# Sparse attention and a bilinear FFN on one core: a fifth pair of seven products, in four PSUM banks

## The chip, the core and the metric

The kernel runs on one core of one Trainium2 chip. The time is the device time of one execution in microseconds; the text works in microseconds from the start of the profiled span where it names a moment. Engines are called PE (TensorE, matmuls), DVE (VectorE), ACT (ScalarE), POOL (GpSimd) and SP (SyncE, which only issues DMAs here). Each engine works through its own queue in the order in which the program wrote it.

## What is computed

Attention for 8 batches of 576 tokens with 8 heads of 64, then a feed-forward block over all 4608 tokens:

```python
scores = scale * np.matmul(q, k.transpose(0, 1, 3, 2))
mask_local = (rel >= 0) & (rel < 32)                    # heads 0 to 3
mask_strided = (rel >= 0) & (pos[None, :] % 32 == pos[:, None] % 32)   # heads 4 to 7
attn = softmax(np.where(mask, scores, -1e9));  x = attn @ v
a = x @ w_a;  b = x @ w_b                               # 512 -> 1536
out = (a * b) @ w_out                                   # 1536 -> 512
```

Matmuls take bf16 inputs and sum in fp32.

## The kernel before

**Tiles and slots.** The 4608 tokens are nine tiles of 512, t = 0 to 8. Each tile has 16 slots: 12 slots f for the columns of a and b (128 features each), then 4 slots for y, the product with w_out. The attention of batch b = t + 1 is cut into small steps that are put between and inside the slots of tile t, in an order that the tables `PAIRED`, `IN_P` and `IN_Y` write out by hand for tiles 2 to 6 (`MID_A`). What a slot issues goes straight into the engines' queues; there is no scheduler behind it.

**A regular slot f** (`ffn_ab`) is four matmuls of 128x128 by 512 tokens for a and four for b, a copy of a on ACT, and a multiplication a * b on DVE into `pf`.

**A pair by seven products** (`a_pair_mid`, pairs g = 0 to 5 are slots 2g and 2g + 1). For two slots, a is a 2x2x2 block product: two blocks of features, two halves of the 512 inputs (256 each), two halves of the tokens. It is done with seven products in place of eight, each of two matmuls of 256 tokens; b stays as it is, with eight matmuls of 512. The products need sums of weight blocks (`wsum_make`, made once in tiles 1 and 2) and of token blocks (`xsum_make`, per tile). Four quarters of a are put together from the products by copies on ACT and adds on DVE; by the numbering in `a_pair`'s plan

    a(0, first half)  = 1 + 2          a(0, second half) = 1 + 6 + 5 + 3
    a(1, first half)  = 1 + 6 + 7 + 4  a(1, second half) = 1 + 6 + 5 + 7

Before, pairs 1 to 4 of tiles 2 to 6 run so, in five PSUM banks: X (products 1, 6, 5, 3 summed up one after the other, and copied out after each), Y (product 2), Z (7, then 4), and b0, b1 for b. Three adds of 256 follow. Pairs 0 and 5 are regular slots.

**PSUM.** Eight banks: three `mm` and one `tp`, handed out in turn by `mm_bank`; `o` and `e`; and `st`, two banks for scores. A bank is given out again when the last reader of its former use is done.

**Attention steps.** `s` makes the scores of a unit u (PE) and their Exp (ACT), `m` masks them (DVE, L417). Units 0 to 3 are local heads, 4 to 7 strided ones. `V` of a strided unit (`step_VT`) multiplies with v into banks `o` and `e` (PE, L519, four matmuls into each), takes Ln of the sums on ACT (L531, one for each bank), Exp of the negative (L532), and multiplies on DVE into `xT` (L534, one for each bank). Units 4 and 5 stand at the ends of slots 9 and 11, unit 6 and 7 inside y.

**The work before y.** y is done by seven products too. `fast_s(t, n, groups)` makes the sums of `pf` for it on DVE (L829): n = 0, 1, 2, 3, for groups of pairs. Sum 1 is made from sum 0. In y, the products run in the order 1, 7, 6, 4, 5, 2, 3; product 1 needs `pf` itself, 7 needs sum 2, 6 needs sum 1.

**POOL** issues the loads of k, q and v; a one-element copy `pace` of the slot's result ahead of a slot's steps holds them back. Other lines named later: L646 and L649 are copy and multiplication of a regular slot, L695 the matmuls of the seven products, L709 those of b, L714 the multiplications, L717 the adds, L721 to L738 the copies, L668 the weight sums, L895 the matmuls of y, L862 and L864 its adds on DVE, L460 the products of a local unit.

Of the kernel before, what the change touches and what calls it, by code (L numbers as in the profile page):

```python
# [7 lines left out]
F32 = mybir.dt.float32  # L8
# [25 lines left out]
def kernel(  # L34
# [10 lines left out]
    nc = tc.nc  # L45
# [218 lines left out]
    def pair_up(nm, c):  # L264

        if (nm, c) == ("k", 1):
            t = shared[1][:96, -RL * 128:]
        else:
            t = blocks(*{"k0": "q0", "q0": "q1", "q1": "k0"}[f"{nm}{c}"])
            t = t.rearrange("p h n -> p (h n)")[:96, :RL * 128]  # L270
        nc.vector.tensor_copy(by_row(t), nats[1, nm, False][:, 2 * c:2 * c + 2])
        paired[1, nm, c] = t.rearrange("p (r m) -> p r m", r=RL)
# [233 lines left out]
        nc.sync.dma_start(out=xT[:, c, S * (b % XR):S * (b % XR + 1)], in_=scratch.pop((b, c)), transpose=True)  # L506

    def step_VT(b, u):

        c, half, M, n, G = unit(u)  # L510
        p = ps.pop((b, u))
        if "e" in psum4:
            o = [psum4[nm].tile([128, 512], F32, tag=nm, name=nm) for nm in "oe"]
        else:
            o2 = psum4["o"].tile([128, 2, 512], F32, tag="o", name="o")
            o = [o2[:, j] for j in range(2)]
        for j in range(2):
            for i in range(G):
                nc.tensor.matmul(o[j][:, i * n:(i + 1) * n], lhsT=vs_buf[b % 2][:, u - HL, 2 * i + j],  # L519
                                 rhs=p_cols(b, p, j, i, n, n)[:M], start=True, stop=True)  # L520
        r = sb.tile([128, RS * 4 * D], BF16, tag="xr", name="xr", bufs=2)[:64, :4 * W].bitcast(F32)
        by_token = lambda t: t.rearrange("d (p i j) -> d p i j", i=G, j=2)
        dst = xT[64 * (u % 2):64 * (u % 2) + 64, c, S * (b % XR):S * (b % XR + 1)]
        if "e" not in psum4:
            by_j = lambda t: t.rearrange("d j (i p) -> d p i j", p=NP)
            nc.scalar.activation(by_token(r), by_j(o2[64:, :, :W]), ACT.Ln)
            nc.scalar.activation(r, r, ACT.Exp, scale=-1.0)
            nc.vector.tensor_mul(by_token(dst), by_j(o2[:64, :, :W]), by_token(r))
            return
        for j in range(2):  # L530
            nc.scalar.activation(by_token(r)[:, :, :, j], o[j][64:, :W].rearrange("d (i p) -> d p i", p=NP), ACT.Ln)  # L531
        nc.scalar.activation(r, r, ACT.Exp, scale=-1.0)  # L532
        for j in range(2):
            nc.vector.tensor_mul(by_token(dst)[:, :, :, j], o[j][:64, :W].rearrange("d (i p) -> d p i", p=NP),  # L534
                                 by_token(r)[:, :, :, j])
# [30 lines left out]
    def F_mm(f, w, kk):  # L566
# [20 lines left out]
             11: "V5"}  # L587
    IN_Y = {2: "S7", 6: "V6", 11: "V7"}
    PAIRED = {-4: "Q0", -3: "Q1", -1: "S0", 0: "S1", 1: "V0 Q2", 2: "s2", 3: "V1 Q3 O0", 4: "s3", 5: "V2", 6: "s4", 7: "V3 O1 I0", 8: "s5",
              9: "V4 I1", 10: "s6", 11: "m6 V5"}  # L590
    IN_P = {1: "m2", 2: "m3", 3: "m4", 4: "m5"}
    FN = {"Tk": step_Tk, "Tq": step_Tq, "S": step_S, "V": step_V, "X": step_X, "W": lambda b, n: fast_w(n, slice(0, 3)),
          "s": S_px, "m": S_m, "L": lead_vl, "O": rows_out, "I": rows_in, "Pk": lambda b, c: pair_up("k", c), "Pq": lambda b, c: pair_up("q", c),
          "Q": lambda b, n: step_Q(b, n // 2, n % 2)}

    def run(b, slot):
# [85 lines left out]
    def a_pair_mid(t, g):  # L682

        pf = pfs[t]
        r = [mm_bank([128, TTOK]) for _ in range(4)]
        r.append(psum4["e"].tile([128, 512], F32, tag="e", name="e"))
        Y, X, Z, b1, b0 = [r[i] for i in ((0, 2, 4, 1, 3), (0, 4, 1, 2, 3), (0, 1, 2, 4, 3))[(g - 1) % 3]]
        X, Y, Z = X[:, :HT], Y[:, :HT], Z[:, :HT]
        a = [fsb.tile([128, TTOK], F32, tag="a_sb", name="a_sb", bufs=4) for _ in range(2)]
        p7 = fsb.tile([128, HT], F32, tag="p7", name="p7")  # L690
        quarter = lambda e, k: a[e][:, HT * k:HT * (k + 1)]

        def P(bank, lhs, rhs, start=False):
            for c in range(2):
                nc.tensor.matmul(bank, lhsT=lhs(c), rhs=rhs(c), start=start and c == 0, stop=c == 1, skip_group_check=True)  # L695

        w = lambda e, j: (lambda c: wav[:, j, c, g, e])
        ws = lambda n: (lambda c: wsum_a[n][:, c, g])
        x = lambda j, k: (lambda c: x_part(t, j, k)[:, c])
        xs = lambda n: (lambda c: xsum[t][:, n, c])  # L700

        def b_mm(bank, e, kks):
            f = 2 * g + e
            x0 = TTOK * t % (XR * S)
            for kk in kks:
                for k in range(2) if x0 + TTOK > XR * S else (None,):
                    rhs = x_part(t, kk // 2, k)[:, kk % 2] if k is not None else xT[:, kk, x0:x0 + TTOK]
                    dst = bank if k is None else bank[:, HT * k:HT * (k + 1)]
                    nc.tensor.matmul(dst, lhsT=wb_sb[:, kk, 128 * f:128 * (f + 1)], rhs=rhs,  # L709
                                     start=kk == 0 and k in (None, 0), stop=kk == KD - 1 and k in (None, 1))  # L710

        def mult(e, bank):
            halves = lambda v_: v_.rearrange("p (a i s) -> p a i s", i=2, s=16)
            nc.vector.tensor_mul(pf[:, 2 * g + e, :].rearrange("p (i a s) -> p a i s", i=2, s=16), halves(a[e]), halves(bank))  # L714

        def add(q, other):
            nc.vector.tensor_tensor(q, other, q, op=ALU.add)  # L717
# [268 lines left out]
    with tc.manual_schedule(engines={ENG.PE, ENG.SP, ENG.Pool, ENG.DVE, ENG.Activation}):  # L986
# [193 lines left out]
```

## Time and profile before

| | us |
|---|---|
| timed runs: median (lowest, highest of 3) | 321.04 (318.89, 322.53) |
| the profiled execution: its time | 318.67 |
| its span in the profile | 317.0 |
| PE busy, in 2770 matmul records | 308.2 |
| DVE busy | 263.7 |
| ACT busy | 198.3 |
| POOL busy | 112.0 |

The granted PE clock is 1.000 over the whole span. Matmul records overlap, since matmuls are pipelined: the time between the starts of two is what one costs. Busy times of DVE and ACT are durations of instructions, and two that follow each other overlap by up to 0.1. Some 28 of 2798 matmuls have no record.

### The profile page before, as it was taken

Reading aid. Unit: us, or ns where it says so; the run is one execution under the profiler, and the core shown is the slowest. Engines: PE = TensorE matmul, PEld = TensorE weight load, DVE = VectorE, ACT = ScalarE, POOL = GpSimd, SP = SyncE. Lnnn points to the kernel's source line nnn. Section 1 sums busy time; section 2 is a strip of 40 time slices with the busy share of each in tenths; the row PEclk is TensorE's granted clock in tenths of the full one; section 3 lists DMA queues with packets and bytes.
Section 4 is the critical chain, followed back from the end, with each engine's and each line's share of the span. In section 5 each row is a group of like instructions: output and inputs, shape, how many; then the busy total and the mean of one; then the engine's idle time right before and its main releaser. Section 6 shows DMA issues by size and latency. Waiting matters only on the chain. (4 is left out here: it accounts for less than half of the span.)

```text
span 317.0 us, 7353 instructions
## 1 busy us (share of the span) xinstructions
PE 308.2 (97%) x2770; PEld 220.6 (70%) x2798; DVE 263.7 (83%) x594; ACT 198.3 (63%) x414; POOL 112.0 (35%) x186
## 2 busy tenths in 40 slices
PE   7899999999999999999999999999999999999994
PEld 6754565455866687767999986769676966786684
DVE  6887876698979998999799978997899768847862
ACT  7964776455766776567666765686667755435541
POOL 8935712772263164115421434133101112203520
PEclk9999999999999999999999999999999999999999
DMA  9999999999799999999999999899352040004004
GB/s 159 168 205 202 203 184 202 216 104 172 127 137 148 223 144 81 127 228 134 108 114 225 118 130 106 202 138 134 30 154 58 0 135 0 2 0 133 2 0 134
DMA packets 127059, 40.32 MB, mean 127 GB/s; under 512 B 114864, under 2 KB 124144, under 8 KB 126832
## 3 DMA queue, kind: packets, MB, share of 16 engines
q0 software_dynamic: 79760, 19.20, 65.2%
q1 hardware_dynamic: 47120, 20.59, 38.8%
q8 instruction: 22, 0.36, 0.5%
q14 instruction: 13, 0.11, 0.1%
q10 hardware_dynamic: 144, 0.07, 0.1%
HBM read 38.93 MB, written 18.28 MB: 181 GB/s over the span
## 5 line engine op out<-in xcount | busy, mean ns | idle before, releaser
L625 PE MATMUL mm<-xT,wb_sb 128*128 128x512 bf16 (+1 forms) x189 | 46.8, 361 | 0.4
L625 PE MATMUL mm<-xT,wa_sb 128*128 128x512 bf16 (+1 forms) x183 | 46.1, 360 | 0.2
L1146 POOL CAST pace<-pf 1x1 f32<-1x1 bf16 x46 | 14.5, 316 | 81.1 <-DVE pf L714 31.6
L399 ACT ACTIVATE p<-st 72x576 bf16<-72x576 f32 (+1 forms) x56 | 36.4, 650 | 9.1 <-PE st L379 8.2
L709 PE MATMUL mm<-xT,wb_sb 128*128 128x512 bf16 (+1 forms) x160 | 38.0, 342 | 0.4
L646 ACT COPY a_sb<-mm 128x512 f32<-128x512 f32 x44 | 25.7, 583 | 15.7 <-PE mm L625 14.9
L895 PEld LDWEIGHTS <-ps 128*128 128x128 bf16 x336 | 32.7, 98 | 3.7
L625 PEld LDWEIGHTS <-wb_sb 128*128 128x128 bf16 x192 | 18.2, 98 | 16.8 <-DVE pf L714 0.3
L895 PE MATMUL mm<-wf,ps 128*128 128x256 bf16 x252 | 29.8, 273 | 0.0
L860 ACT COPY y_sb<-mm 128x512 f32<-128x512 f32 (+1 forms) x32 | 17.9, 558 | 19.0 <-PE mm L895 16.4
L649 DVE TENSOR_TENSOR pf<-a_sb,mm 128x512 bf16<-128x512 f32 x34 | 23.1, 680 | 5.9 <-ACT a_sb L646 5.8
L625 PEld LDWEIGHTS <-wa_sb 128*128 128x128 bf16 x192 | 17.4, 98 | 12.4
L1146 POOL COPY pace<-y_sb 1x1 f32<-1x1 f32 x22 | 8.4, 380 | 49.9 <-DVE y_sb L858 27.3
L895 PEld LDWEIGHTS <-pf 128*128 128x128 bf16 x252 | 23.5, 98 | 2.7
L775 PE MATMUL mm<-xT,wb_sb 128*128 128x512 bf16 x83 | 25.3, 379 | 0.1
L709 PEld LDWEIGHTS <-wb_sb 128*128 128x128 bf16 x192 | 18.7, 97 | 7.4
L238 POOL DMA_DIRECT2D vs<-in_v_dram x24 | 21.7, 907 | 3.9 <-ACT y_sb L860 1.3
L714 DVE TENSOR_TENSOR pf<-a_sb,mm 128x512 bf16<-128x512 f32 x35 | 22.7, 683 | 0.5
L895 PE MATMUL mm<-wo_sb,pf 128*128 128x256 bf16 x168 | 21.8, 273 | 0.0
L829 DVE TENSOR_TENSOR ps<-pf 128x512 bf16<-128x512 bf16 (+2 forms) x37 | 17.8, 481 | 0.7
L460 PEld LDWEIGHTS <-p 128*128 128x128 bf16 (+1 forms) x256 | 12.9, 97 | 5.2 <-DVE p L417 1.3
L417 DVE TENSOR_TENSOR p<-p,mask_l 128x576 int16<-128x576 int16 x32 | 14.4, 451 | 2.2 <-ACT p L399 2.0
(222 smaller groups left out, 734.2 us busy)
## 6 DMA issues: line engine op xcount, KB each, us to landing
out_dram<-y_sb SPq DMA_DIRECT2D x14, 512.0 KB, 4.8
kr<-in_k_dram POOLq DMA_DIRECT2D x12, 288.0 KB, 6.1
qr<-in_q_dram POOLq DMA_DIRECT2D x12, 288.0 KB, 8.1
vl<-in_v_dram POOLq DMA_DIRECT2D x6, 384.0 KB, 6.9
out_dram<-y_sb SPq DMA_DIRECT2D x7, 256.0 KB, 4.3
vs<-in_v_dram POOLq DMA_DIRECT2D x24, 72.0 KB, 5.7
xd<-xl SPq DMA_DIRECT2D x12, 144.0 KB, 4.0
wo_sb<-in_moe_w_out_dram POOLq DMA_DIRECT2D x4, 384.0 KB, 11.7
```

The costliest lines, as they stand in the source:

```text
L238: nc.gpsimd.dma_start(out=vs_buf[b % 2][:, h, :, 0:D], in_=v[b, HL + h].rearrange("(p r) d -> p r d", r=RS))
L399: nc.scalar.activation(p_flat(p)[:M, :2 * W].rearrange("p (i n) -> p i n", n=2 * n), st[:M].rearrange("p a (i n) -> p (a i) n", n=256)[:, ...
L625: nc.tensor.matmul(ps_[:, c0:c0 + n], lhsT=w[:, kk, 128 * f:128 * (f + 1)], rhs=xT[:, kk, x0:x0 + n], start=(kk == first and c0 == 0), sto ...
L646: nc.scalar.copy(a_sb, ab[0])
L649: nc.vector.tensor_mul(pf[:, f, :].rearrange("p (i a s) -> p a i s", i=2, s=16), halves(a_sb), halves(ab[1]))
L709: nc.tensor.matmul(dst, lhsT=wb_sb[:, kk, 128 * f:128 * (f + 1)], rhs=rhs, start=kk == 0 and k in (None, 0), stop=kk == KD - 1 and k in (N ...
L714: nc.vector.tensor_mul(pf[:, 2 * g + e, :].rearrange("p (i a s) -> p a i s", i=2, s=16), halves(a[e]), halves(bank))
L775: nc.tensor.matmul(got[e], lhsT=wb_sb[:, kk, 128 * f:128 * (f + 1)], rhs=xT[:, kk, x0:x0 + TTOK], start=kk == 0, stop=kk == KD - 1)
L829: nc.vector.tensor_tensor(s[:, n], a, b, op=op)
L860: nc.scalar.copy({"1": part(0, 0), "7": part(0, 1), "6": part(1, 0), "5": part(1, 1)}[k], bank)
L895: nc.tensor.matmul(bank[b][:, q], lhsT=lhs(g, q), rhs=rhs(g), start=k in "172" and q == 0 and g == 0, stop=g == FG - 1, skip_group_check=True)
L1146: nc.gpsimd.tensor_copy(pace, done)
```

## The change

- **Pair 5** of tiles 2 to 6 becomes a pair by seven products like pairs 1 to 4. The weight sums for pair 5, so far made in tile 2's y, are made with those of pairs 1 to 4 in tile 1.
- **Four banks.** Products 2 and 5 go side by side into one bank W, product 3 onto 5. X takes 1, 6, 7 and 4, summed up and copied out after each. One add of 512 (W onto a(0)) and one of 256 (u3 = 1 + 6 + 7 onto a(1)) replace the three adds. The first half of the pair now does b0 with the products 1, 2, 5, 6, 3, 7, the second half b1 with product 4; the multiplication for feature block 0 (`mult(0, b0)`) stands at the start of the second half. Bank `e` serves pairs 1 to 3 alone. Which bank has which part is written out for each pair.
- **Strided unit 4 in parts**: `u` (products and the two Ln) at the end of slot 9, `x` (Exp) inside pair 5 behind the copy of product 6, `n` (the two multiplications on DVE, which free banks `o` and `e`) at the end of slot 10. The other strided units call the three parts one after the other.
- **Sums for y**: sum 1 of groups 0 to 3 moves from slot 10 to slot 9, behind sum 2 of these groups; sum 2 of groups 4 and 5 moves into pair 5, behind `mult(0, b0)`.

```diff
-MID_A = {t: (1, 2, 3, 4) for t in (2, 3, 4, 5, 6)}
+MID_A = {t: (1, 2, 3, 4, 5) for t in (2, 3, 4, 5, 6)}
...
     def step_VT(b, u):
+        VT_p(b, u)
+        VT_x(b, u)
+        VT_n(b, u)
...
+    def VT_x(b, u):
+        r = held[b, "vt", u][3]
         nc.scalar.activation(r, r, ACT.Exp, scale=-1.0)
+
+    def VT_n(b, u):
+        by_token, dst, o, r = held.pop((b, "vt", u))
...
         for j in range(2):
             nc.vector.tensor_mul(by_token(dst)[:, :, :, j], o[j][:64, :W].rearrange("d (i p) -> d p i", p=NP),
                                  by_token(r)[:, :, :, j])
...
-              9: "V4 I1", 10: "s6", 11: "m6 V5"}
+              9: "u4 I1", 10: "n4 s6", 11: "m6 V5"}
...
-        r = [mm_bank([128, TTOK]) for _ in range(4)]
-        r.append(psum4["e"].tile([128, 512], F32, tag="e", name="e"))
-        Y, X, Z, b1, b0 = [r[i] for i in ((0, 2, 4, 1, 3), (0, 4, 1, 2, 3), (0, 1, 2, 4, 3))[(g - 1) % 3]]
+        r = {x: psum4["e"].tile([128, 512], F32, tag="e", name="e") if x == "e" else mm_bank([128, TTOK])
+             for x in ("012e", "30e1", "e230", "1230", "1230")[g - 1]}
+        X, W, b0, b1 = [r[x] for x in ("1e02", "e301", "320e", "2103", "1203")[g - 1]]
...
-        P(Y, w(0, 1), x(1, 0), True)
         P(X, w(0, 0), x(0, 0), True)
         nc.scalar.copy(quarter(0, 0), X)
-        b_mm(b1, 1, (0, 1, 2))
+        P(W[:, :HT], w(0, 1), x(1, 0), True)
+        P(W[:, HT:], ws(0), xs(0), True)
+        nc.scalar.copy(quarter(1, 1), W[:, HT:])
+        b_mm(b0, 0, (0, 1))
         P(X, ws(1), xs(1))
+        nc.scalar.copy(quarter(0, 1), X)
+        take(("q", t, g))
+        b_mm(b0, 0, (2, 3))
+        P(W[:, HT:], ws(3), x(1, 1))
+        nc.vector.tensor_tensor(a[0], W, a[0], op=ALU.add)
+        P(X, ws(2), xs(2))
+        nc.scalar.copy(u3, X)
+        yield u3[:1, :1]
+        mult(0, b0)
+        if g == FG - 1:
+            fast_s(t, 2, slice(4, 6))
+        b_mm(b1, 1, (0, 1))
+        P(X, w(1, 1), xs(3))
         nc.scalar.copy(quarter(1, 0), X)
-        P(Z, ws(2), xs(2), True)
-        nc.scalar.copy(p7, Z)
-        b_mm(b1, 1, (3,))
-        add(quarter(0, 0), Y)
-        yield p7[:1, :1]
-        P(X, ws(0), xs(0))
-        nc.scalar.copy(quarter(1, 1), X)
-        P(Z, w(1, 1), xs(3))
-        add(quarter(1, 0), Z)
-        b_mm(b0, 0, range(KD))
+        b_mm(b1, 1, (2, 3))
+        nc.vector.tensor_tensor(quarter(1, 1), u3, quarter(1, 1), op=ALU.add)
         take(("p", t, g))
-        add(quarter(1, 1), p7)
-        P(X, ws(3), x(1, 1))
-        nc.scalar.copy(quarter(0, 1), X)
         mult(1, b1)
-        mult(0, b0)
-        if g == 4:
+        if g == FG - 2:
             fast_s(t, 0, slice(0, 4))
...
+                if b - 1 in MID_A:
+                    steps["q", b - 1, 5] = [(b, ["x4"])]
...
-            if t not in FAST_A:
+            if t not in FAST_A and t not in MID_A:
                 soon[16 * t + 10] = [lambda t=t: fast_s(t, 2, slice(4, 6))]
...
-            do((17, 17, 18, 19)[n], wsum_make, n, slice(1, 5))
-            do(16 * 2 + 12 + n, wsum_make, n, slice(0, 6, 5))
+            do((17, 17, 18, 19)[n], wsum_make, n, slice(1, 6))
+            do(16 * 2 + 12 + n, wsum_make, n, slice(0, 1))
...
-                    ((8, 0, 0, 4),) if t == 1 else ()) + ((9, 2, 0, 4), (10, 1, 0, 4), (12, 3, 0, 6)) if t == 1 or t in MID_A else ((4, 0, 0, 2), (5, 2, 0, 2), (6, 1, 0, 2), (7, 3, 0, 2), (8, 2, 2, 4), (9, 0, 2, 4),
+                    ((8, 0, 0, 4),) if t == 1 else ()) + ((9, 2, 0, 4), (10 if t == 1 else 9, 1, 0, 4), (12, 3, 0, 6)) if t == 1 or t in MID_A else ((4, 0, 0, 2), (5, 2, 0, 2), (6, 1, 0, 2), (7, 3, 0, 2), (8, 2, 2, 4), (9, 0, 2, 4),
```

More of the change, by code (lines that the diff above doesn't have):

```diff
@@ L508, in step_VT, with VT_p @@
     def step_VT(b, u):
+        VT_p(b, u)
+        VT_x(b, u)
+        VT_n(b, u)
+    def VT_p(b, u):
         c, half, M, n, G = unit(u)
@@ L523, in step_VT @@
         dst = xT[64 * (u % 2):64 * (u % 2) + 64, c, S * (b % XR):S * (b % XR + 1)]
+        held[b, "vt", u] = by_token, dst, o, r
         if "e" not in psum4:
@@ L526, in step_VT @@
             nc.scalar.activation(by_token(r), by_j(o2[64:, :, :W]), ACT.Ln)
-            nc.scalar.activation(r, r, ACT.Exp, scale=-1.0)
-            nc.vector.tensor_mul(by_token(dst), by_j(o2[:64, :, :W]), by_token(r))
+            held[b, "vt", u] = by_token, dst, (by_j(o2[:64, :, :W]),), r
             return
@@ L531, in step_VT @@
             nc.scalar.activation(by_token(r)[:, :, :, j], o[j][64:, :W].rearrange("d (i p) -> d p i", p=NP), ACT.Ln)
+    def VT_x(b, u):
+        r = held[b, "vt", u][3]
         nc.scalar.activation(r, r, ACT.Exp, scale=-1.0)
+    def VT_n(b, u):
+        by_token, dst, o, r = held.pop((b, "vt", u))
+        if len(o) == 1:
+            nc.vector.tensor_mul(by_token(dst), o[0], by_token(r))
+            return
         for j in range(2):
@@ L589 @@
     PAIRED = {-4: "Q0", -3: "Q1", -1: "S0", 0: "S1", 1: "V0 Q2", 2: "s2", 3: "V1 Q3 O0", 4: "s3", 5: "V2", 6: "s4", 7: "V3 O1 I0", 8: "s5",
-              9: "V4 I1", 10: "s6", 11: "m6 V5"}
+              9: "u4 I1", 10: "n4 s6", 11: "m6 V5"}
     IN_P = {1: "m2", 2: "m3", 3: "m4", 4: "m5"}
     FN = {"Tk": step_Tk, "Tq": step_Tq, "S": step_S, "V": step_V, "X": step_X, "W": lambda b, n: fast_w(n, slice(0, 3)),
-          "s": S_px, "m": S_m, "L": lead_vl, "O": rows_out, "I": rows_in, "Pk": lambda b, c: pair_up("k", c), "Pq": lambda b, c: pair_up("q", c),
+          "s": S_px, "m": S_m, "u": VT_p, "x": VT_x, "n": VT_n, "L": lead_vl, "O": rows_out, "I": rows_in, "Pk": lambda b, c: pair_up("k", c), "Pq": lambda b, c: pair_up("q", c),
           "Q": lambda b, n: step_Q(b, n // 2, n % 2)}
@@ L684, in a_pair_mid @@
         pf = pfs[t]
-        r = [mm_bank([128, TTOK]) for _ in range(4)]
-        r.append(psum4["e"].tile([128, 512], F32, tag="e", name="e"))
-        Y, X, Z, b1, b0 = [r[i] for i in ((0, 2, 4, 1, 3), (0, 4, 1, 2, 3), (0, 1, 2, 4, 3))[(g - 1) % 3]]
-        X, Y, Z = X[:, :HT], Y[:, :HT], Z[:, :HT]
+        r = {x: psum4["e"].tile([128, 512], F32, tag="e", name="e") if x == "e" else mm_bank([128, TTOK])
+             for x in ("012e", "30e1", "e230", "1230", "1230")[g - 1]}
+        X, W, b0, b1 = [r[x] for x in ("1e02", "e301", "320e", "2103", "1203")[g - 1]]
+        X = X[:, :HT]
         a = [fsb.tile([128, TTOK], F32, tag="a_sb", name="a_sb", bufs=4) for _ in range(2)]
-        p7 = fsb.tile([128, HT], F32, tag="p7", name="p7")
+        u3 = fsb.tile([128, HT], F32, tag="p7", name="p7")
         quarter = lambda e, k: a[e][:, HT * k:HT * (k + 1)]
@@ L714, in mult @@
             nc.vector.tensor_mul(pf[:, 2 * g + e, :].rearrange("p (i a s) -> p a i s", i=2, s=16), halves(a[e]), halves(bank))
-        def add(q, other):
-            nc.vector.tensor_tensor(q, other, q, op=ALU.add)
-        P(Y, w(0, 1), x(1, 0), True)
         P(X, w(0, 0), x(0, 0), True)
         nc.scalar.copy(quarter(0, 0), X)
-        b_mm(b1, 1, (0, 1, 2))
+        P(W[:, :HT], w(0, 1), x(1, 0), True)
+        P(W[:, HT:], ws(0), xs(0), True)
+        nc.scalar.copy(quarter(1, 1), W[:, HT:])
+        b_mm(b0, 0, (0, 1))
         P(X, ws(1), xs(1))
-        nc.scalar.copy(quarter(1, 0), X)
-        P(Z, ws(2), xs(2), True)
-        nc.scalar.copy(p7, Z)
-        b_mm(b1, 1, (3,))
-        add(quarter(0, 0), Y)
-        yield p7[:1, :1]
-        P(X, ws(0), xs(0))
-        nc.scalar.copy(quarter(1, 1), X)
-        P(Z, w(1, 1), xs(3))
-        add(quarter(1, 0), Z)
-        b_mm(b0, 0, range(KD))
+        nc.scalar.copy(quarter(0, 1), X)
[11 more added lines that the diff above has]
+        P(X, w(1, 1), xs(3))
+        nc.scalar.copy(quarter(1, 0), X)
+        b_mm(b1, 1, (2, 3))
+        nc.vector.tensor_tensor(quarter(1, 1), u3, quarter(1, 1), op=ALU.add)
         take(("p", t, g))
-        add(quarter(1, 1), p7)
-        P(X, ws(3), x(1, 1))
-        nc.scalar.copy(quarter(0, 1), X)
         mult(1, b1)
-        mult(0, b0)
-        if g == 4:
+        if g == FG - 2:
             fast_s(t, 0, slice(0, 4))
@@ L1069 @@
                 for g in MID_A.get(b - 1, ()):
-                    steps["p", b - 1, g] = [(b, IN_P[g].split())]
+                    steps["p", b - 1, g] = [(b, IN_P.get(g, "").split())]
+                if b - 1 in MID_A:
+                    steps["q", b - 1, 5] = [(b, ["x4"])]
                 for n, names in IN_Y.items():
```

## The prediction

> **What bounds the kernel now.** I read the page first, then the busy time of the five changed tiles, then VectorE (DVE) and TensorE (PE) in order of time. The page:
>
> ```profile
> span 317.0 us, 7353 instructions
> ...
> PE 308.2 (97%) x2770; PEld 220.6 (70%) x2798; DVE 263.7 (83%) x594; ACT 198.3 (63%) x414; POOL 112.0 (35%) x186
> ```
>
> PE is the bound; DVE is the next fullest. Tiles t = 2 to 6, from one tile's first matmul to the next tile's, by busy time in each stretch (PE, weight load, DVE, ScalarE (ACT), GpSimd):
>
> ```profile
> 81.40:114.20 32.80, 32.64 (x287) 23.51 (x288) 30.24 (x64) 22.11 (x48) 13.34 (x21) 1.00 1.38 152
> 114.20:147.29 33.09, 32.93 (x289) 23.87 (x290) 31.25 (x71) 22.58 (x50) 11.47 (x19) 1.00 1.42 145
> 147.29:180.20 32.91, 32.91 (x353) 29.84 (x352) 29.84 (x67) 22.24 (x50) 11.41 (x19) 1.00 1.36 142
> ```
>
> PE is busy for all of it (a missing matmul record is 0.2), at clock 1.00: each matmul less is time saved, each PE wait is time lost. DVE has 2 to 3 us to spare per tile, so the order of its queue matters. It runs like this from pair 4 of tile t = 3, whose first product starts at 138.24:
>
> ```profile
> 140.94 0.42 DVE L717 TENSOR_TENSOR a_sb<-e,a_sb 128x256 f32<-128x256 f32 x1 [0.23 <-PE e L695]
> 141.28 0.45 DVE L417 TENSOR_TENSOR p<-p,mask_s 72x576 int16<-72x576 int16 x1
> 141.65 0.41 DVE L717 TENSOR_TENSOR a_sb<-p,a_sb 128x256 f32<-128x256 f32 x1
> 142.09 1.28 DVE L714 TENSOR_TENSOR pf<-a_sb,mm 128x512 bf16<-128x512 f32 x2
> 143.30 0.68 DVE L829 TENSOR_TENSOR ps<-pf 128x1024 bf16<-128x1024 bf16 x1
> 143.90 0.47 DVE L534 TENSOR_TENSOR xT<-o,xr 64x288 bf16<-64x288 f32 x1
> 144.27 0.46 DVE L534 TENSOR_TENSOR xT<-e,xr 64x288 bf16<-64x288 f32 x1
> 144.64 0.67 DVE L829 TENSOR_TENSOR ps<-pf 128x1024 bf16<-128x1024 bf16 x1
> 145.23 0.67 DVE L649 TENSOR_TENSOR pf<-a_sb,mm 128x512 bf16<-128x512 f32 x1
> 145.94 0.42 DVE L829 TENSOR_TENSOR ps<-pf 128x512 bf16<-128x512 bf16 x1
> 146.28 0.68 DVE L829 TENSOR_TENSOR ps<-ps,pf 128x1024 bf16<-128x1024 bf16 x1
> ```
>
> The two L534 rows free banks o and e of strided unit 4 and end at 144.73. Unit 5 takes both banks; its products on PE:
>
> ```profile
> 145.72 0.29 PE L519 MATMUL o<-p,vs 72*128 72x72 bf16 x4
> ```
>
> That is 0.99 later: today PE does not wait. All depends on what becomes of this 0.99.
>
> **What the change gives.** PE rates from the same view: eight matmuls of 512 columns take 142.01 to 143.74, 0.216 each; 24 of 256 take 147.54 to 150.16, 0.109 each. Pair 5 goes from 16 x 0.216 = 3.46 to 14 x 0.109 + 8 x 0.216 = 3.25: 0.20 a tile, **-1.03** in five tiles (tile 4, whose matmuls are all halves, gives 0.22). Pairs 1 to 4 keep their matmuls.
>
> **Pairs 1 to 4 in four banks.** Positions from the pair's first matmul: product 1 at 0, 2 at 0.22, 5 at 0.44, two b matmuls, 6 at 1.09, two b, 3 at 1.74, 7 at 1.95, the score unit (0.25), two b, 4 at 2.85, two b until 3.50. Bank X is copied out three times before a product is added to it. A copy starts 0.31 after the start of a product's second matmul (138.57 to the L721 copy at 138.88), takes 0.37, and 0.05 behind a copy PE went on without a gap (140.40 to 140.45). Product 7: 1.20 + 0.31 + 0.37 + 0.05 = 1.93 against 1.95, no wait. Product 4: 2.06 + 0.31 + 0.42 = 2.79 against 2.85; where the copy of u3 also waits for POOL (pairs 2 and 3 in the built order), I take 0.38 in place of 0.31, as the L717 row shows for two waits (140.56 to 140.94), and 2.87 is 0.02 late: 10 x 0.02 = **+0.2**, bounds 0 and 0.07 x 10 = 0.7. Banks from pair to pair are free in time: the latest is b1, freed at 4.25 + 0.69 + 0.05 = 4.99 (below), and only pair 5 after pair 4 takes the same bank again at once, at 3.76 + 2.42.
>
> DVE's adds go from three of 256 (0.34 from start to start) to one of 512 (0.69 as L864, 0.61 to the next start) and one of 256: 0.07 less per pair, off the bound.
>
> The Trainium skill, Perfetto Trace Analysis, section Matmul Optimizations, asks for all eight PSUM banks to be used; the change takes one away from the pair. By that rule the pair waits on its copies; the rows above leave 0.02 to 0.06 of cover, so that case is the third rival below.
>
> **Unit 4 in parts and the queue behind it.** In the built order DVE does, from pair 4 on: add a0 (512), mult 0, add u3, mask m5, mult 1, fast_s 0, 2 and 1 of groups 0 to 3, add a0 of pair 5, unit 4's two multiplications. Fast_s 2 and 1 now stand ahead of unit 4, and so does pair 5's add. The add a0 can start at 1.85 (second matmul of product 3) + 0.38 = 2.23; DVE is free by then (pair 3's last, unit 3's 128-row normalisation, ends at 1.94 by the same rows). Start to start, from the rows above: 0.72 (0.69 and 0.03 to a reader of its result), 0.60, 0.34, 0.37, 0.60, 0.60, 0.59, 0.60, 0.61, 0.37, and 0.46 for the last: 5.86. Unit 4 ends at **8.09**. A PE weight load went on 0.05 after the mask it waited for (71.43 to 71.48 in tile 1).
>
> PE: pair 4 is 3.50, unit 4's products 0.26 (141.75 to 142.01), pair 5 3.50, unit 5's 0.26: unit 5 would end at 7.51. With bank e free at 8.14 and its four matmuls of 0.03, it ends at 8.27: a wait of 0.76 in each tile, **+3.8** in five. Behind it on PE stands all of y. Bounds: 0, if DVE's ten steps were 0.76 shorter; 1.1, if two-wait starts (0.07 each) added to five of them.
>
> ACT in pair 5: unit 4's two Ln (0.43 and 0.41) end at 4.57, where the copy of product 1 was ready at 4.25; product 6 waits 0.19. The Exp (0.69) ahead of u3's copy makes product 4 wait 0.21. Both lie ahead of unit 5, and its wait shrinks by as much: nothing in the sum while DVE ends last, 0.40 a tile if it doesn't.
>
> Then in y: the matmul that needs pf of f = 10 comes at 8.27 + 0.55 = 8.82; mult 0 is ready at 8.73. Fast_s 2 and 1 of pair 5 end at 9.14 and 11.11, needed at 10.26 and 11.57. Unit 6 follows at 12.44, its banks free at 12.40. No further wait, though with little cover. Behind unit 6 DVE waits for its Exp as before (0.70 idle in tile 2's y), so nothing is carried into the next tile. POOL's and SP's queues keep their DMAs in order; POOL's extra reading of u3 holds back no load, and the vs loads, which wait for unit 5's matmuls, come 0.8 later for use a tile later.
>
> **Weight sums of pair 5.** Four subtractions in tile 1 go from 1024 to 1280 elements: rows of 512, 1024 and 1536 are 0.42, 0.68 and 0.94, so 0.13 each, 0.52. Nothing covers them: DVE has no idle time there from 58.3 to 73.7, and PE's weights wait for DVE's masks:
>
> ```profile
> PEld L460 <- DVE p L417: 1.3, 3, 0.6
> ```
>
> Two of the three are units 1 and 2 of tile 1 (PE stood 0.29 and 0.09). **+0.52**, bounds 0 and 0.52. What is saved in tile 2's y lies off the bound.
>
> **Sum.** -1.03 + 0.2 + 3.8 + 0.52 = +3.5. The profiled execution took 318.67 (span 317.0), so 322.2; the median of the three timed runs is 321.04, 2.4 above it, and I give the time on that scale: **324.5**, 1.1% slower.
>
> **Rivals.**
> Not slower (other side): DVE frees bank e before PE asks for it. It decides in pair 5: unit 4 would have to end by 7.33 in place of 8.09, and ACT's Ln and Exp would have to fit between the copies. For it: DVE has 3 us to spare in the tile. Against: ten steps in a row with no idle time. If DVE alone is early, ACT's 0.40 is left: 5 x 0.20 + 0.2 + 0.52 = +1.7, 322.8. If both are hidden and tile 1's too: 320.2.
> Dearer bank chain: if the two-wait start holds for all copies, products 7 and 4 wait 0.05 and 0.02 in 20 pairs, and unit 6, with 0.04 of cover, 0.1 a tile: +2 more, 326.5.
> Clock: stalls of 0.8 could lower it. Rows: 1.00 in all stretches, tile 1's stalls of 0.29 included. If a tenth of each changed tile's y (11) ran at half speed, 5 x 1.1 = +5.5 more, 330. The Trainium skill, TensorE: Matmul & The Clock Gate, section on psum-queue depth-cycling, tells of a kernel whose short idle times between groups made the clock swing; no run here shows such a stall.
> That pair 5 does not become a seven-product pair is excluded: the built order has its 14 short matmuls.
>
> **How the numbers follow.** Forecast 0.66; ACT alone 0.12; all hidden 0.08; bank chain 0.12; clock 0.02. A measurement of this kernel tells about 1% (3.2) from no change. The forecast's own bounds are +2.5 to +5, some six tenths of it above 3.2, since the covers left out can only add: slower 0.40 + 0.14 = 0.54, same 0.44, faster 0.02. The range for 8 in 10 takes the forecast's bounds, ACT alone and the bank chain (322.8 to 326.5), with 1 either way since the three timed runs lie up to 2 from their median: 321.6 to 327.4.
>
> **What would show it.** Tiles 2 to 6 each 33.4 to 33.5 long against 32.9; weight loads of the strided unit's line waiting for DVE's xT rows, 0.3 to 0.8 in each of five tiles; the xT rows of unit 4 behind a 512-wide add; DVE later by 0.5 in tile 1. I am wrong if unit 5's loads do not wait, if waits stand at products 4, 6 or 7 alone, or if the granted clock falls.

## The result and the profile after

The changed kernel takes **322.47 us** (median of 22 runs, 321.27 to 327.75). The kernel before takes 319.24 over as many runs, 1.8 lower than the median of the three that the forecast was put on. The ratio, worked out from runs of the two kernels side by side, is **1.0107, with a 95% interval of 1.0082 to 1.0132** (the medians alone give 1.0101): slower, by just about the 1% that the prediction took for the least that can be told from no change. The difference of the medians is 3.2; the forecast's sum was +3.5. The profiled execution took 321.62 against 318.67.

The page of the changed kernel:

```profile
span 319.9 us, 7452 instructions
...
PE 311.1 (97%) x2820; PEld 222.8 (70%) x2820; DVE 267.7 (84%) x584; ACT 201.9 (63%) x429; POOL 110.5 (35%) x185
```

PE is as full as it was, DVE one per cent fuller: the page alone does not say where 3 us went. So I cut the span into tiles, from the first weight load of a tile's slot 0 to that of the next tile. (The stretches shown in the prediction were cut some 9 us earlier, inside y; that moves a tile's length by up to 0.2.) The profiled executions of the kernels below reach tile 1 at 55.7 to 56.4 or at 58.7 to 59.7, the same kernel at 55.7 once and at 59.1 once (e10 and e4 below), so kernels are compared from the start of tile 1 on. Busy time by stretch, before: tile 3 and tile 1; the columns are PE, weight load, DVE, ACT, POOL, granted clock, DMA share, GB/s.

```profile
123.22:156.09 32.87, 32.71 (x287) 23.67 (x289) 30.42 (x69) 22.36 (x49) 11.63 (x20) 1.00 1.40 145
...
55.94:90.27 34.33, 34.04 (x269) 21.39 (x270) 29.97 (x56) 20.11 (x34) 16.64 (x27) 1.00 1.41 153
```

The same of the changed kernel: tiles 2, 3 and 4, and last tile 1.

```profile
90.57:124.01 33.44, 33.16 (x296) 24.31 (x295) 30.80 (x67) 23.08 (x52) 13.29 (x24) 1.00 1.60 162
124.01:157.45 33.44, 33.16 (x297) 24.32 (x296) 30.90 (x66) 23.02 (x52) 11.47 (x20) 1.00 1.35 142
157.45:191.00 33.55, 33.30 (x353) 29.78 (x352) 30.67 (x65) 23.05 (x52) 10.88 (x19) 1.00 1.45 142
55.77:90.57 34.80, 34.36 (x271) 21.33 (x269) 30.43 (x56) 20.12 (x34) 16.86 (x27) 1.00 1.31 146
```

Tiles 2 to 6 are longer by 0.49, 0.57, 0.51, 0.56 and 0.56, tile 1 by 0.47, and the rest from tile 7 on is the same (62.31 against 62.35). Together that is 3.12, at a granted clock of 1.00 in each stretch. DVE has 0.5 to 0.9 more to do per tile and still 2.5 or more to spare in it.

What waits is shown by the waits of PE and of its weight loads in the changed kernel (total, times, longest; "issue" is where the view found no releaser):

```profile
PE o L524 <- DVE xT L548: 1.3, 5, 0.3
...
PEld L524 <- issue: 3.4, 5, 0.7
PEld L460 <- DVE p L417: 1.8, 3, 0.8
PEld L709 <- issue: 1.3, 5, 0.3
```

L524 is the matmuls of the strided units, L709 those of the seven products. Both stand there five times, once a tile. L460, the products of the local units, waits for masks; that row went from 1.3 to 1.8, and what was added stands in tile 1.

VectorE in order of time, from pair 4 of tile 3, whose first product starts at 139.04:

```profile
141.27 0.69 DVE L741 TENSOR_TENSOR a_sb<-mm,a_sb 128x512 f32<-128x512 f32 x1 [0.28 <-PE mm L709]
141.99 0.69 DVE L728 TENSOR_TENSOR pf<-a_sb,mm 128x512 bf16<-128x512 f32 x1
142.60 0.42 DVE L752 TENSOR_TENSOR a_sb<-p,a_sb 128x256 f32<-128x256 f32 x1
142.93 0.45 DVE L417 TENSOR_TENSOR p<-p,mask_s 72x576 int16<-72x576 int16 x1
143.30 0.68 DVE L728 TENSOR_TENSOR pf<-a_sb,mm 128x512 bf16<-128x512 f32 x1
143.90 1.28 DVE L843 TENSOR_TENSOR ps<-pf 128x1024 bf16<-128x1024 bf16 x2
145.10 0.68 DVE L843 TENSOR_TENSOR ps<-ps,pf 128x1024 bf16<-128x1024 bf16 x1
145.71 0.68 DVE L741 TENSOR_TENSOR a_sb<-mm,a_sb 128x512 f32<-128x512 f32 x1
146.31 0.46 DVE L548 TENSOR_TENSOR xT<-o,xr 64x288 bf16<-64x288 f32 x1
146.67 0.47 DVE L548 TENSOR_TENSOR xT<-e,xr 64x288 bf16<-64x288 f32 x1
```

After the first 0.28 there is no idle time in ten steps (the group x2 counts two). The two L548 rows free banks o and e of unit 4; they end at 147.14, 8.10 after the pair's start. On PE, unit 5's matmuls into the same banks, and the first of y behind them:

```profile
146.05 0.59 PE L723 MATMUL mm<-xT,wb_sb 128*128 128x512 bf16 x2
146.92 0.29 PE L524 MATMUL o<-p,vs 72*128 72x72 bf16 x4 [0.27 <-DVE xT L548]
147.19 0.30 PE L524 MATMUL e<-p,vs 72*128 72x72 bf16 x4
147.33 0.93 PE L909 MATMUL mm<-wo_sb,pf 128*128 128x256 bf16 x7
```

Two matmuls of 512 from 146.05 leave PE free at 146.48; the next starts at 146.92, 0.43 later. (The 0.27 in brackets is counted from the end of a matmul's record, which runs on after the next matmul could start.) From the first matmul into o to the first into e there are 0.28 (the rows are rounded) in place of the 0.13 that four of them took before, 0.15 late. With 0.16 to 0.18 at product 6 that makes 0.73 to 0.76 of waiting per changed tile, and there is no other wait over 0.03 in it.

### The profile page after: what moved, and what is told of

It reads as the page before. It is cut to its first block, busy times and chain, and to the rows that moved or that the text cites. A ratio compares the mean times of both kernels' runs of the same rounds, so it can differ in the third digit from the quotient of the medians.

```text
span 319.9 us, 7452 instructions
## 1 busy us (share of the span) xinstructions
PE 311.1 (97%) x2820; PEld 222.8 (70%) x2820; DVE 267.7 (84%) x584; ACT 201.9 (63%) x429; POOL 110.5 (35%) x185
## 4 chain that ended last, share of the span: by engine, by line
PE 84%; DVE 9%; issue 2%; DMA 2%; POOL 2%; ACT 0%; DVEq 0%; POOLq 0%
PE mm L909 20%; PE mm L639 17%; PE mm L723 8%; PE mm L709 7%; PE mm L789 6%; PE st L379 3%; PE mm L971 3%; PE ax L782 3%; PE o L460 2%; PE e L709 2%; PE mm L782 2%; DVE a_sb L741 2%; DMA shared<-in_q_dram 2%; DVE pf L728 2%; DVE ps L843 2%
## 5 line engine op out<-in xcount | busy, mean ns | idle before, releaser
L723 PE MATMUL mm<-xT,wb_sb 128*128 128x512 bf16 (+1 forms) x216 | 53.6, 343 | 0.0
L639 PE MATMUL mm<-xT,wa_sb 128*128 128x512 bf16 (+1 forms) x144 | 37.1, 367 | 0.0
L639 PE MATMUL mm<-xT,wb_sb 128*128 128x512 bf16 (+1 forms) x144 | 37.1, 367 | 0.0
L1162 POOL CAST pace<-pf 1x1 f32<-1x1 bf16 x41 | 12.3, 301 | 62.2 <-DVE pf L728 36.4
L728 DVE TENSOR_TENSOR pf<-a_sb,mm 128x512 bf16<-128x512 f32 x45 | 30.7, 682 | 1.3
L660 ACT COPY a_sb<-mm 128x512 f32<-128x512 f32 x34 | 19.8, 584 | 15.0 <-PE mm L639 14.9
L789 PE MATMUL mm<-xT,wb_sb 128*128 128x512 bf16 x88 | 26.2, 379 | 0.0
L663 DVE TENSOR_TENSOR pf<-a_sb,mm 128x512 bf16<-128x512 f32 x24 | 16.3, 681 | 6.0 <-ACT a_sb L660 6.0
L639 PEld LDWEIGHTS <-wa_sb 128*128 128x128 bf16 x144 | 13.2, 98 | 10.3
L460 PEld LDWEIGHTS <-p 128*128 128x128 bf16 (+1 forms) x256 | 12.9, 97 | 8.1 <-DVE p L417 1.8
L709 PEld LDWEIGHTS <-tq 128*128 128x128 bf16 x100 | 9.8, 98 | 10.5 <-issue 1.3
```

Source lines behind the costliest of these rows:

```text
L460: nc.tensor.matmul(of[:, j, i, :w], lhsT=pt, rhs=vt, start=True, stop=True)
L639: nc.tensor.matmul(ps_[:, c0:c0 + n], lhsT=w[:, kk, 128 * f:128 * (f + 1)], rhs=xT[:, kk, x0:x0 + n], start=(kk == first and c0 == 0), sto ...
L660: nc.scalar.copy(a_sb, ab[0])
L789: nc.tensor.matmul(got[e], lhsT=wb_sb[:, kk, 128 * f:128 * (f + 1)], rhs=xT[:, kk, x0:x0 + TTOK], start=kk == 0, stop=kk == KD - 1)
L1162: nc.gpsimd.tensor_copy(pace, done)
```

## The experiments

All kernels are edits of the changed one. The table gives the length of tile 1, of tiles 2 to 6, and from tile 1 to the end, each from one profiled execution, then the median time and its ratio to the kernel before, run beside it. The ratio is not the quotient of two times in the table: the kernel before, run beside the edits, had medians from 319.17 to 320.84. Lengths of stretches with the same work agree within 0.1 (e4 aside, see there), far closer than the times.

| kernel | tile 1 | tiles 2 to 6 | to the end | time | ratio, 95% |
|---|---|---|---|---|---|
| before | 34.33 | 164.34 | 261.02 | 319.24 | 1 |
| changed | 34.80 | 167.03 | 264.14 | 322.47 | 1.0107 (1.0082, 1.0132) |
| e1 sum 1 on POOL | 34.80 | 164.56 | 261.68 | 320.24 | 1.0043 (0.9996, 1.0090) |
| e2 sum 1 behind unit 4 | 34.80 | 167.00 | 264.13 | 321.79 | 1.0095 (1.0079, 1.0110) |
| e3 four banks alone | 34.33 | 164.28 | 260.93 | 319.05 | 0.9994 (0.9961, 1.0027) |
| e4 weight sums late | 34.32 | 167.44 | 264.07 | 323.95 | 1.0092 (1.0026, 1.0157) |
| e10 the same again | 34.33 | 167.12 | 263.84 | 321.28 | 1.0047 (1.0010, 1.0085) |
| e5 unit 4 whole | 34.80 | 167.66 | 264.87 | 324.44 | 1.0141 (1.0078, 1.0204) |
| e6 sum 2 twice | 34.80 | 170.76 | 267.87 | 327.15 | 1.0244 (1.0200, 1.0288) |
| e7 e1 and e4 | 34.32 | 164.57 | 261.21 | 318.80 | 0.9944 (0.9891, 0.9997) |
| e9 a Ln moved | 34.80 | 167.03 | 264.23 | 321.58 | 1.0055 (0.9993, 1.0116) |
| e8 e7 and e9 | 34.32 | 164.09 | 260.76 | 318.78 | 0.9965 (0.9916, 1.0015) |

The theory to be tested: unit 5 waits for DVE's queue, step for step. Rivals: the order of that queue alone, ACT, the four banks.

### e1: one step fewer in VectorE's queue

Sum 1 of groups 0 to 3 is made by POOL.

```diff
-        nc.vector.tensor_tensor(s[:, n], a, b, op=op)
+        (nc.gpsimd if t in MID_A and n == 1 and gs.start == 0 else nc.vector).tensor_tensor(s[:, n], a, b, op=op)
```

> The changed kernel with sum 1 of groups 0 to 3 (0.60 of DVE's queue ahead of unit 4) on POOL in tiles 2 to 6. DVE-queue theory: unit 4's multiplications end 0.60 earlier, so unit 5's wait on PE (0.43 + 0.15 a tile) falls to 0 to 0.1 and y's load of the last pf block does not wait; five tiles give -2.6 to -2.9, a ratio to before of 1.001 to 1.003. What stays is the wait of product 6 in pair 5 (0.17 a tile). Rival, that ACT's Ln and Exp or the four banks set unit 5's start: no change, ratio 1.010 to 1.011. If POOL takes more than some 4 us for the sum, or its loads come late behind it, y's products 6 wait instead.

The five tiles lose 2.47, 0.49 each, a little less than the 2.6 to 2.9 that I expected, and the wait for bank o is gone. Product 6 still waits 0.17 and bank e 0.08 to 0.09. DVE and PE in order of time:

```profile
147.36 1.28 DVE L843 TENSOR_TENSOR ps<-pf 128x1024 bf16<-128x1024 bf16 x2
148.66 0.69 DVE L741 TENSOR_TENSOR a_sb<-mm,a_sb 128x512 f32<-128x512 f32 x1
149.27 0.46 DVE L548 TENSOR_TENSOR xT<-o,xr 64x288 bf16<-64x288 f32 x1
149.64 0.47 DVE L548 TENSOR_TENSOR xT<-e,xr 64x288 bf16<-64x288 f32 x1
```

```profile
148.17 0.38 PE L709 MATMUL mm<-xT,tq 128*128 128x256 bf16 x2
...
149.94 0.29 PE L524 MATMUL o<-p,vs 72*128 72x72 bf16 x4
150.16 0.30 PE L524 MATMUL e<-p,vs 72*128 72x72 bf16 x4
150.30 1.48 PE L909 MATMUL mm<-wo_sb,pf 128*128 128x256 bf16 x12
```

One step is 0.60, the gain 0.49, and the rest can be seen: pair 5's add (L741) no longer starts where the queue lets it, 2 x 0.60 after 147.36 = 148.56, but at 148.66. That is product 3's second matmul, 0.11 after 148.17, and 0.38. So the last 0.08 to 0.09 is a chain from product 3 through the add of pair 5 and unit 4 back to PE. The queue was the bound of unit 5's wait for all but that.

### e2: the same step, behind unit 4 in place of ahead of it

```diff
-(10 if t == 1 else 9, 1, 0, 4)
+(10, 1, 0, 4)
```

> The changed kernel with sum 1 of groups 0 to 3 back at the end of slot 10, behind unit 4's multiplications and ahead of mult 0. DVE-queue theory, DVE full in this stretch: unit 5's wait goes (0.58 a tile), but mult 0 of pair 5 ends where it did, and y's sixth weight load, which now comes 0.58 earlier, waits some 0.5 for it; -0.1 a tile, ratio 1.008 to 1.010. Rival, that the order alone is at fault: all of the 0.58 a tile is won, -2.9, ratio 1.001 to 1.002.

Nothing is won: 264.13 against 264.14. Unit 5's wait goes as in e1, and y waits in its place:

```profile
147.25 0.71 PE L909 MATMUL mm<-wo_sb,pf 128*128 128x256 bf16 x5
148.28 0.50 PE L909 MATMUL mm<-wo_sb,pf 128*128 128x256 bf16 x3 [0.31 <-DVE pf L728]
```

Five matmuls of 0.11 end at 147.80; the sixth needs `pf` of pair 5 and starts 0.48 later. Between unit 4's multiplications and `pf`'s (L728), DVE now has the sum that was put back:

```profile
146.59 0.46 DVE L548 TENSOR_TENSOR xT<-e,xr 64x288 bf16<-64x288 f32 x1
146.96 0.67 DVE L843 TENSOR_TENSOR ps<-ps,pf 128x1024 bf16<-128x1024 bf16 x1
147.55 0.67 DVE L728 TENSOR_TENSOR pf<-a_sb,mm 128x512 bf16<-128x512 f32 x1
```

So the order ahead of unit 4 is not the fault by itself: from pair 4 into y, DVE has one step more than fits.

### e6: one step more

Sum 2 of groups 0 to 3 is made twice in tiles 2 to 6, the second time over the first.

```diff
+                if t in MID_A and (n, z0, z1) == (2, 0, 4):
+                    do(16 * t + slot, fast_s, t, n, slice(z0, z1))
```

> The changed kernel with sum 2 of groups 0 to 3 made twice, one after the other, in tiles 2 to 6: 0.60 more in DVE's queue ahead of unit 4, PE and ACT as they were. DVE-queue theory: unit 5 waits 0.60 longer in each of five tiles, +3.0, ratio 1.019 to 1.022. Rival, ACT or banks: no change, ratio 1.010 to 1.012.

Tiles 3 to 6 grow by 0.71 to 0.73 each (tile 2 by 0.87, with two small waits of its own). The second write did not cost the 0.60 that I had expected:

```profile
144.81 0.68 DVE L843 TENSOR_TENSOR ps<-pf 128x1024 bf16<-128x1024 bf16 x1
145.41 1.41 DVE L843 TENSOR_TENSOR ps<-pf 128x1024 bf16<-128x1024 bf16 x2
146.73 0.69 DVE L843 TENSOR_TENSOR ps<-ps,pf 128x1024 bf16<-128x1024 bf16 x1
```

Sum 0 starts at 144.81, sum 2 at 145.41, 0.60 later. The second making of sum 2 ends 1.41 after that and takes 0.69, so it starts 0.71 to 0.72 after the first; sum 1 follows it in 0.6 again. All of this arrives in PE's wait for bank o, which goes from 0.41 to 0.44 up to 1.13 to 1.16 (1.14 in tile 3, from 147.40 on):

```profile
146.97 0.59 PE L723 MATMUL mm<-xT,wb_sb 128*128 128x512 bf16 x2
148.54 0.29 PE L524 MATMUL o<-p,vs 72*128 72x72 bf16 x4 [0.98 <-DVE xT L548]
```

One step more on DVE is therefore paid in full; one step less (e1) gave 0.49 of its 0.60.

### e3: the four banks alone

Pairs 1 to 4 keep their new form in four banks, while pair 5, unit 4, the sums for y (sum 2 of groups 4 and 5 in slot 10 again) and the weight sums are as before.

```diff
-MID_A = {t: (1, 2, 3, 4, 5) for t in (2, 3, 4, 5, 6)}
+MID_A = {t: (1, 2, 3, 4) for t in (2, 3, 4, 5, 6)}
...
-              9: "u4 I1", 10: "n4 s6", 11: "m6 V5"}
+              9: "V4 I1", 10: "s6", 11: "m6 V5"}
...
-(10 if t == 1 else 9, 1, 0, 4)
+(10, 1, 0, 4)
...
-            do((17, 17, 18, 19)[n], wsum_make, n, slice(1, 6))
-            do(16 * 2 + 12 + n, wsum_make, n, slice(0, 1))
+            do((17, 17, 18, 19)[n], wsum_make, n, slice(1, 5))
+            do(16 * 2 + 12 + n, wsum_make, n, slice(0, 6, 5))
```

> The kernel before with the new four-bank pair for pairs 1 to 4 alone: pair 5 regular, unit 4 whole at slot 9, sums for y and weight sums as before. DVE-queue theory: the four-bank pair costs nothing (product 7 has 0.02 and product 4 about 0.05 of cover), ratio 0.998 to 1.002, and PE has no gap over 0.03 in pairs 1 to 4. Rival, the bank chain: products 7 and 4 wait 0.05 or more in each pair, 20 pairs, +1 or more, ratio 1.003 or more.

```profile
126.00:158.87 32.87, 32.87 (x290) 23.75 (x289) 30.26 (x65) 22.73 (x49) 11.47 (x20) 1.00 1.34 143
```

That is tile 3 in the columns of above: 32.87, as before, and PE has no wait over 0.03 in tiles 2 to 6. The four banks cost nothing and gain nothing.

### e5: unit 4 in one piece

```diff
-              9: "u4 I1", 10: "n4 s6", 11: "m6 V5"}
+              9: "V4 I1", 10: "s6", 11: "m6 V5"}
...
-                if b - 1 in MID_A:
-                    steps["q", b - 1, 5] = [(b, ["x4"])]
```

> The changed kernel with unit 4 whole at the end of slot 9: Ln, Ln and Exp in a row on ACT, its multiplications on DVE ahead of sums 2 and 1. DVE-queue theory: banks o and e are free at 6.3 of pair 4's clock, long before unit 5, whose wait goes; but the copy of product 1 of pair 5 comes 0.6 to 0.7 later behind the Exp, and product 6 waits 0.8 to 0.9 in place of 0.17. 0 to 0.15 a tile more than the changed kernel, ratio 1.010 to 1.014. Rival, that cutting unit 4 in parts is what costs: the 0.58 a tile goes, -2.9, ratio 1.001 to 1.003.

0.13 a tile worse than the changed kernel. Unit 5 doesn't wait any more, but product 6 of pair 5 does, 0.88 to 0.89, for ACT's copy of product 1, which stands behind unit 4's Ln and Exp:

```profile
145.35 0.38 PE L709 MATMUL mm<-xsum,tq 128*128 128x256 bf16 x2 [0.72 <-ACT a_sb L731]
```

So cutting unit 4 in parts is not what costs. It trades a wait of 0.88 for ACT for 0.76 of waits for ACT and DVE.

### e9: ACT taken away alone

Unit 4's second Ln goes behind the copy of product 1 in pair 5.

```diff
-        for j in range(2):
-            nc.scalar.activation(by_token(r)[:, :, :, j], o[j][64:, :W].rearrange("d (i p) -> d p i", p=NP), ACT.Ln)
+        VT_l(b, u, 0)
+        if u != 4 or b - 1 not in MID_A:
+            VT_l(b, u, 1)
...
         nc.scalar.copy(quarter(0, 0), X)
+        take(("l", t, g))
...
+                    steps["l", b - 1, 5] = [(b, ["l4"])]
```

> The changed kernel with unit 4's second Ln behind the copy of product 1 of pair 5, nothing else. DVE-queue theory: product 6's wait of 0.17 goes and unit 5's grows by as much, since DVE frees banks o and e when it did; 0.76 a tile in all as before, ratio 1.0107. Rival, that ACT's chain counts by itself: -0.17 a tile, -0.85, ratio 1.008.

By tiles it is the changed kernel to 0.01 in each. Product 6 waits no longer (0.07 and 0.06 are left at products 3 and 7), and unit 5 waits 0.47 and 0.15: the sum is 0.75 in tile 3.

```profile
148.96 0.59 PE L728 MATMUL mm<-xT,wb_sb 128*128 128x512 bf16 x2
149.86 0.29 PE L524 MATMUL o<-p,vs 72*128 72x72 bf16 x4 [0.31 <-DVE xT L553]
```

ACT's wait costs nothing while DVE ends last, since unit 5 waits that much less. The measured ratio came out at 1.0055, whose interval includes the 1.0107 that I expected.

### e4 and e10: the weight sums later

Pair 5's weight sums are made in tile 1's y. e10 is the same kernel run again.

```diff
-            do((17, 17, 18, 19)[n], wsum_make, n, slice(1, 6))
+            do((17, 17, 18, 19)[n], wsum_make, n, slice(1, 5))
+            do(16 + 12 + n, wsum_make, n, slice(5, 6))
```

> The changed kernel with the weight sums of pair 5 made in tile 1's y (four subtractions of 256 elements after its slots), where DVE has idle time, in place of 0.13 more on each of four subtractions at the start of tile 1. Theory of the weight sums: the PE wait of 0.49 at unit 0 of tile 1 goes, those at units 1 and 2 stay as in the kernel before (0.29 and 0.09); -0.47 against the changed kernel, ratio to before 1.009. Rival, that DVE's lateness in tile 1 comes from elsewhere: the waits stay, ratio 1.0107.

> The kernel with pair 5's weight sums in tile 1's y once more, since its profile had a wait of 0.42 at unit 0 of tile 2 for a load of v beside the 0.48 won in tile 1. If that wait belongs to the one execution: tiles 1 to 5 at 34.3, 33.4, 33.4, 33.5, 33.4 and 0.48 less than the changed kernel from tile 1 to the end. If the moved sums cause it: tile 2 at 33.9 again, and nothing won.

Tile 1 is back at 34.32 and 34.33 in both. But in e4's profiled execution tile 2 lost 0.42, waiting for a load of v:

```profile
PE o L460 <- DMA vl<-in_v_dram: 0.3, 1, 0.3
```

In e10's tile 2 there is a wait of 0.12 at another place, and in e7 and e8, which hold the same edit, there is none. So the 0.47 of tile 1 is DVE's time for the weight sums, as forecast. The times can't show a gain of this size: the ratios of e4 and e10, the same kernel, are 1.0092 and 1.0047. The traces tell more of the load. POOL issues it at the same point in all four, 27.9 after the start of tile 1, and it lands 10.6 later in e4, 8.9 in e10, 7.9 in e7 and 10.2 in e8. PE could have used it 38.1 after the start of tile 1; in e4 it landed at 38.5. In the changed kernel tile 1 is 0.47 longer, and the same load landed at 38.5 just before PE came to it. So nothing shows that the moved sums delay the load. They bring PE to it earlier, and an execution in which it lands late gives the gain back. What makes its time vary, no run here shows.

### e7 and e8: all causes taken away together

e7 has the edits of e1 and e4, e8 that of e9 as well.

> Sum 1 of groups 0 to 3 on POOL and the weight sums of pair 5 in tile 1's y, together. By the sum: -1.03 for pair 5, 5 x 0.26 for product 6 and unit 5's bank e, nothing in tile 1: +0.2 against the kernel before, ratio 0.999 to 1.002. If the two gains do not add up, 1.003 or more.

> As the run with both, and unit 4's second Ln on ACT put behind the copy of product 1 of pair 5, which product 6 waits for. Product 6's wait of 0.17 goes; PE then reaches unit 5 earlier by that, and DVE, full from pair 4 on, frees bank e 0.1 to 0.2 after it is asked for: 0.15 to 0.2 a tile is left of 0.26. -1.03 + 0.8 to 1.0 = -0.2 to 0, ratio 0.998 to 1.001. Rival, that ACT sets the pair: 0.26 a tile goes entirely, -1.0, ratio 0.997.

```profile
123.56:156.42 32.86, 32.86 (x297) 24.38 (x295) 30.29 (x65) 23.14 (x52) 13.72 (x21) 1.00 1.34 142
```

In e8's tile 3 the view has PE busy for the whole 32.86 (waits under 0.1 are hidden by the records, which overlap). In e7 product 6 and bank e keep waits of 0.16 to 0.18 and 0.08 to 0.09, and e7 needs 0.19 more than the kernel before, where 0.2 were worked out. Product 6's wait is the one for ACT that cost nothing in e9: without DVE's queue behind it, it counts, and e8 takes 0.45 off. It doesn't take all of it, since the Ln that was moved now stands ahead of the copies that products 3 and 7 wait for. From tile 1 to the end e8 needs 260.76, 0.26 less than the kernel before. Pair 5 alone saves 1.03 of matmuls; waits of some 0.16 a tile (0.07 and 0.06 at products 3 and 7, 0.03 at bank e) take 0.8 of it back. By time it is 0.9965 of the kernel before, with an interval that includes 1: as fast, not shown to be faster. e7's interval lies just below 1, though its profile is 0.19 longer from tile 1 on; I don't take that for a gain.

## Why the prediction was right

The time, the sign and the place were as forecast: 322.47 lies in the range, and the ratio that the forecast stood for, 324.5 to 321.04, is 1.0108 against 1.0107. That the two agree to the fourth place is luck: the interval is 0.0025 to either side, and the terms of the sum were off by 0.05 to 0.2. The scale was off too: the median of three runs was 1.8 too high, so that 322.47, taken as a bare time, is nearer to the rival's 322.8 than to 324.5. What tells the two apart is the difference to the kernel before (+3.2, where the forecast had +3.5 and that rival +1.7) and the waits. Point by point:

- **Pair 5's matmuls, -1.03**: borne out by e8, whose saving and remaining waits add up to it within 0.1 (0.26 and 0.8).
- **Unit 5's wait, 0.76 a tile, +3.8**: 0.73 to 0.76 in each tile with product 6's wait in it, 3.76 in all. Unit 4's end was worked out at 8.09 and is 8.10. That DVE's queue sets it was shown by taking a step away (e1) and adding one (e6); that there is no free place behind unit 4 by e2. One thing the prediction left out: it found mult 0 ready at 8.73 against 8.82 in y, a cover of only 0.09, so it could have said that moving a sum back would make y wait, as e2 did.
- **Products 6 and 4 in pair 5**: product 6 was to wait 0.19 and waits 0.16 to 0.18. Product 4 was to wait 0.21 and doesn't. The step that failed is the spacing on ACT: I let every instruction start 0.02 or more after the end of the one ahead, and here the Exp and u3's copy start before it:

```profile
144.48 0.37 ACT L737 COPY a_sb<-mm 128x256 f32<-128x256 f32 x1 [0.19 <-PE mm L709]
144.75 0.68 ACT L540 ACTIVATE xr<-xr 64x576 f32<-64x576 f32 x1
145.41 0.37 ACT L743 COPY p<-mm 128x256 f32<-128x256 f32 x1
```

  By the forecast's spacing the Exp (L540) would start at 144.87 at the earliest and u3's copy (L743) at 145.57. The Exp starts 0.10 before the copy of product 6 ends, and is then out of the way: u3's copy starts 0.36 after product 7's second matmul, as it does in pairs 2 and 3, which have no Exp there. It made no difference to the sum, since the wait for unit 5 took up whatever ACT left, as the forecast said of both and e9 shows for product 6.
- **Products 4 and 7 in pairs 1 to 4, +0.2**: no such wait; 0. The 0.38 that I took for the start of u3's copy is the time that adds on DVE take to start after a matmul (the row was one of DVE). The copies of u3 start 0.31 after product 7's second matmul, and 0.36 in eight of the ten of pairs 2 and 3; by the forecast's own sum that makes 2.84 against 2.85, just in time. e3 shows the same for four banks at large, and with it the third rival (326.5) falls. The Trainium skill asks in Perfetto Trace Analysis, section Matmul Optimizations, to have all eight PSUM banks in use. No run here tests that, since both kernels use all eight; that a pair holds four of them in place of five cost 0 of 164 us in e3.
- **Weight sums, +0.52**: 0.47 in tile 1. The four subtractions went from 0.68 to 0.82 each:

```profile
60.41 0.82 DVE L682 TENSOR_TENSOR tk<-wa_sb 128x1280 bf16<-128x1280 bf16 x1
```

  That is +0.13 to 0.14 each, 0.5 in all, and nearly all of it reached PE, as three waits of 0.49, 0.27 and 0.09 where two of 0.29 and 0.09 were; e4 and e10 take it back.
- **Sum**: with the measured terms, -1.03 + 3.76 + 0.47 = +3.20; the stretch from tile 1 to the end grew by 3.12 (the kernel before had a wait of 0.07 in tile 2 that the changed one doesn't have). The forecast's +3.5 was 0.2 too high by products that don't wait and 0.05 by the weight sums.
- **Clock rival (330)**: PE stood still for 0.43, 0.15 and 0.17 in each changed tile, and the granted clock is 1.00 in all of them. (It shows 0.98 only from tile 7 to the end, where nothing was changed and the length is as before.) The depth-cycling that the Trainium skill tells of (TensorE: Matmul & The Clock Gate, A second HAM failure mode) did not come with three stalls in 33 us, nor with e5's single stall of 0.88 in each tile. What stalls of this size would do if they came closer together, no run here shows.
- **Not slower (322.8 with DVE alone early, 320.2 with all hidden, both on the scale that was 1.8 too high)**: did not happen by itself, but e1, e7 and e8 make this rival true step by step: DVE alone taken away leaves +0.66 from tile 1 on (the rival's +1.7 had ACT's 0.40 a tile in it, of which the 0.21 of product 4 doesn't occur), all three leave -0.26.

## What to carry to other kernels

An engine with 2.5 us to spare in a tile of 33 can still have no free step in the 6 us that matter: add up its queue instruction by instruction between the two events that PE waits for, and compare with PE's own time to the same point. Moving a step behind the one that frees a bank helps only if the next consumer has room for it; otherwise the wait moves along (e2), and what took it away here was less work on that engine, with the step on another one that was idle there (e1). When one wait is removed, the next late engine counts at once, so list the covers beneath it before counting the gain.

## What the runs showed of the hardware

- **POOL beside DVE.** The sum of 128x1024 bf16 that takes DVE 0.68 took POOL 2.14 to 2.44 (e1). The spread follows DVE: POOL started while DVE was still in its own sum from two SBUF inputs, which had 0.31 to 0.45 to go in four tiles and 0.07 in tile 5, and less that overlap the durations are 1.99 (2.07 in tile 5). So POOL seems to have stood still until DVE's sum was done. DVE's next instructions, each with one input in PSUM, kept their 0.69, 0.46, 0.47 and 0.66 while POOL ran:

```profile
148.32 2.31 POOL L843 TENSOR_TENSOR ps<-ps,pf 128x1024 bf16<-128x1024 bf16 x1
```

  This agrees with the Trainium skill, SBUF — State Buffer, Who interferes with whom: a DVE instruction with two SBUF inputs contends with a GpSimd one that reads SBUF, and one with at most one SBUF input does not, outside modes in which DVE uses both of its ports. Had POOL's sum been put beside DVE's own sums of y, it could by that rule have held them up; no run here shows that.
- **ACT** starts an instruction that has nothing else to wait for between 0.11 before and 0.03 after the end of the one ahead (changed kernel). Unit 4's Exp starts 0.10 before the end of a copy whose result it doesn't need, and a unit's Exp 0.03 after the end of the Ln whose result it needs. But that is not the whole rule: the copy of product 1 in pair 5 starts 0.02 after the end of unit 4's second Ln, and doesn't need it. What else decides, no run here shows.
- **DVE** started a second write to the same place 0.71 to 0.72 after the first, where a write to another place took 0.60 (e6).
- **Loads of v** vary: the one for tile 2, issued at the same point after the start of tile 1, took 7.9 to 10.6 to land in four executions (e4, e7, e8, e10), and PE waited 0.42 for the slowest.
